# Loading and placing a table in two lots, and adding all row blocks of the output weight on GpSimd

## Chip, cores, metric

One core of a Trainium2 chip. The metric is the device time of one execution, in microseconds (us); "time" below is that, and "span" is the profiled execution from first to last instruction, some 1.5 to 2 us shorter.

## The reference, cut to what matters

```python
# x (8, 3008, 256), w_r/w_i (256, 256), w_in (256, 2048), w_out (2048, 256)
X  = rfft(x, axis=1)
Yr = Xr @ w_r - Xi @ w_i + b_r ;  Yi = Xr @ w_i + Xi @ w_r + b_i
Y  = soft-threshold(Yr, Yi, 0.01)
y  = irfft(Y)                       # (8, 3008, 256)
h  = relu(y @ w_in);  out = (s * h*h + b) @ w_out
```

The constant `b` contributes `b * (column sums of w_out)` to every row. The kernel computes that once, as a bias.

## The kernel before

The FFT over 3008 = 94 x 32 points is done with matmuls. Batch 0 goes first and alone, so its steps wait for each other: a first transform of the eight pieces of x (`ut`), a mix with the weights (`g`), a forward transform with tables `F_t` and `F_2`, relu steps (`m`, `z`), an inverse transform, transposes, a last transform. Mix, forward and inverse steps go in units of four pairs of frequencies; the result of each is copied out of PSUM by ScalarE or VectorE, which is called an eviction here. Then the big matmuls with `w_in` and `w_out` begin, with the later batches woven in. The tables of the first 12 of 24 pairs of frequencies come compactly (`F_c`) and are spread on the chip into zeroed blocks:

```python
    def emit_load_forward():
        nc.sync.dma_start(out=F_c.rearrange("p q r k -> p q (r k)"), in_=F_d)   # 192 KB
        nc.sync.dma_start(out=sel_t, in_=S_d)
    ...
    def place_f():                      # ScalarE
        for a in range(2):
            r = slice(64 * a, 64 * a + 64)
            nc.scalar.copy(out=blocks(F_t)[r, 0:H, :, a], in_=F_c[r])
    def place_f_2():                    # VectorE
        for a in range(2): ...          # two copies, two negations, 64x384 each
    ...
    # first_batch
        for g in range(8):              # two groups per chunk c of x, h = 0, 1
            ...                         # 8 matmuls on a piece of x, two evictions into ut
            last_pe = keep_awake(5)     # five filler matmuls
            if h == 0: continue
            if c == 0:
                with tc.issue_after(last_dve.ins):
                    nc.vector.memset(F_c[0:1, 0, 0, 0:1], 0.0)   # gate for the load
                emit_load_forward()
            ...
        with tc.issue_after(last_dve.ins), tc.issue_after(last_act.ins):
            place_f()
            place_f_2()
        ...
        for i in range(2 * U + 2):
            if i < 2 * U:          mix(*steps[i])
            if 0 <= i - 1 < 2 * U: fwd_dft(*steps[i - 1])
            if 0 <= i - 2 < 2 * U: inv_dft(*steps[i - 2])
```

`w_out` is loaded in two parts (12 and 4 of its 16 row blocks). GpSimd adds the first 12 blocks into two (`w_sum`, five adds), and six matmuls with a matrix of ones sum the rest over the partitions:

```python
    def make_bias():
        parts = [w_out_t[:, q] for q in range(12, MC)] + [w_sum[:, 0], w_sum[:, 1]]
        for i, part in enumerate(parts):
            nc.tensor.matmul(ps[:, 0:D], ones, part, ...)
        nc.scalar.activation(out=bias_bc, in_=ps[:, 0:D], func=AF.Copy, scale=bb_bc)
```

## Time and profile before

| | kernel before |
|---|---|
| time, first session | 847.06 us (846.77 to 847.17, 3 runs) |
| profiled span | 845.9 us (this execution took 847.72 us) |
| TensorE busy | 835.2 us, 99% |
| first mix matmul / first w_in matmul / first use of `us` | 14.39 / 46.05 / 62.97 us |

The three times of the last row are the marks: they cut the start into a stretch that x sets (to 14.39), the dependent steps of batch 0 (to 46.05) and the stretch in which the bias is made (to 62.97). The prediction shows the chain of waits and TensorE's timeline there. One line of the same timeline is needed further: the first inverse transform.

```profile
19.80 0.40 PE L478 MATMUL psa<-T_t,z 128*128 128x128 f16 x4
```

### The profile page before, as it was taken

The page shows a single profiled execution, that of the slowest core. Times are in us where ns is not written, and L with a number is a line of the kernel's source. Part 1 is how long each engine was busy: PE and PEld are TensorE (multiplying, and loading weights), DVE is VectorE, ACT ScalarE, POOL GpSimd, SP SyncE. Part 2 cuts the span into 40 slices and gives each one's busy share as a digit, 9 for nine tenths or more (in the row PEclk, how much of TensorE's full clock was granted, in tenths as well). Part 3 has the DMA queues.
Part 4 walks back from the last instruction along what each step waited for, and adds up shares of the span by engine and source line. Part 5 has one row for each costly group of instructions (what it writes and reads, how often), then busy time and mean ns, then how long its engine had stood idle before and what let it go on. Part 6 is the DMA issues. An engine that isn't in the chain of part 4 may idle for free.

```text
span 845.9 us, 17109 instructions
## 1 busy us (share of the span) xinstructions
PE 835.2 (99%) x6658; PEld 600.6 (71%) x6658; DVE 693.8 (82%) x1027; ACT 641.3 (76%) x862; POOL 42.9 (5%) x69
## 2 busy tenths in 40 slices
PE   8999999999999999999999999999999999999997
PEld 6857767777677767777677776777767777766765
DVE  5989987888888987888888888798978888776674
ACT  5988887778778877787777787778877778666673
POOL 4430000000000001000000000000000000000000
PEclk9999999999999999999999999999999999999999
DMA  8955467224762367324761247613354223411111
GB/s 199 175 153 121 117 161 205 68 73 102 194 163 57 101 166 197 85 73 107 189 173 50 81 100 198 168 44 90 102 155 122 61 79 97 112 33 38 38 44 50
DMA packets 105762, 96.06 MB, mean 114 GB/s; under 512 B 9558, under 2 KB 97498, under 8 KB 104338
## 3 DMA queue, kind: packets, MB, share of 16 engines
q1 hardware_dynamic: 99218, 80.55, 33.0%
q0 software_dynamic: 6464, 14.42, 10.6%
q8 instruction: 52, 0.85, 0.4%
q14 instruction: 28, 0.23, 0.1%
HBM read 53.52 MB, written 46.66 MB: 118 GB/s over the span
## 4 chain that ended last, share of the span: by engine, by line
PE 91%; DMA 3%; ACT 3%; DVE 2%; issue 1%; POOL 0%; DVEq 0%; ACTq 0%; POOLq 0%
PE psh L782 37%; PE psa L853 37%; PE psf L648 4%; PE psf L583 3%; PE psf L634 2%; PE psf L619 2%; PE psf L678 2%; PE psf L731 2%; ACT rt L789 1%; DMA ud<-u 1%; PE psm L430 1%; DMA x<-in_x_dram 1%; DMA F_c<-dft_fwd 1%; PE psf L460 0%; DMA ring<-ring 0%
## 5 line engine op out<-in xcount | busy, mean ns | idle before, releaser
L789 ACT ACTIVATE rt<-psh 128x1024 f32<-128x1024 f32 (+2 forms) x384 | 387.0, 1009 | 120.3 <-PE psh L782 119.1
L796 DVE TENSOR_TENSOR gt<-rt 128x1024 f16<-128x1024 f32 (+2 forms) x319 | 382.2, 1201 | 94.7 <-ACT rt L789 93.6
L853 PE MATMUL psa<-w_out_t,gt 128*128 128x256 f16 (+1 forms) x3024 | 454.1, 272 | 0.1
L853 PEld LDWEIGHTS <-gt 128*128 128x128 f16 (+1 forms) x3024 | 301.0, 101 | 186.1 <-issue 1.1
L782 PE MATMUL psh<-yt,w_in 128*128 128x512 f16 (+1 forms) x1344 | 396.6, 378 | 0.2 <-ACT rt L789 0.2
L782 PEld LDWEIGHTS <-w_in 128*128 128x128 f16 x1536 | 142.8, 98 | 26.3 <-issue 1.0
L863 DVE SCALAR_TENSOR_TENSOR ost<-psa,s_bc,bias_bc 128x512 f32<-128x512 f32 (+2 forms) x97 | 71.1, 733 | 9.6 <-PE psa L853 8.0
L793 ACT ACTIVATE gt<-rt 128x1024 f16<-128x1024 f32 (+2 forms) x65 | 68.2, 1050 | 1.0
L653 DVE TENSOR_TENSOR ring<-psf,s 128x512 f16<-128x512 f32 x84 | 57.5, 684 | 3.2 <-PE psf L648 2.9
L170 ACT CAST v<-psf 128x512 f16<-128x512 f32 x77 | 44.9, 582 | 19.3 <-PE psf L678 19.3
L170 ACT CAST xf<-psf 128x512 f16<-128x512 f32 x79 | 46.3, 586 | 9.4 <-PE psf L619 9.4
L782 PE MATMUL psh<-tail,w_in 128*128 128x512 f16 (+1 forms) x192 | 52.1, 353 | 0.0
L170 ACT CAST u<-psf 96x512 f16<-96x512 f32 x74 | 42.8, 580 | 11.3 <-PE psf L583 11.0
L648 PE MATMUL psf<-W_g,xf 128*128 128x256 f16 x336 | 50.4, 272 | 0.0
L170 ACT CAST yt<-psf 128x480 f16<-128x480 f32 (+2 forms) x76 | 38.9, 519 | 14.8 <-PE psf L731 14.2
L213 POOL DMA_DIRECT2D x<-in_x_dram x36 | 18.7, 526 | 433.2 <-PE psf L583 432.0
L583 PE MATMUL psf<-x,A_t 94*96 94x512 f16 x102 | 38.9, 382 | 1.0 <-ACT yt L170 0.6
L659 DVE TENSOR_TENSOR ring<-ring,high 128x512 f16<-128x512 f16 x84 | 35.5, 423 | 2.3
L660 DVE TENSOR_TENSOR ring<-ring 128x512 f16<-128x512 f16 x84 | 35.5, 423 | 2.1
L658 DVE TENSOR_TENSOR ring<-ring,low 128x512 f16<-128x512 f16 x84 | 35.4, 421 | 1.6
L648 PEld LDWEIGHTS <-xf 128*128 128x128 f16 x336 | 32.9, 98 | 4.1 <-issue 0.2
L731 PE MATMUL psf<-C_t,vs 96*128 96x96 f16 x448 | 33.2, 205 | 0.0
(99 smaller groups left out, 503.5 us busy)
## 6 DMA issues: line engine op xcount, KB each, us to landing
out_dram<-ost SPq DMA_DIRECT2D x152, 128.0 KB
ud<-u SPq DMA_DIRECT2D x28, 384.0 KB
us<-ud SPq DMA_DIRECT2D x28, 384.0 KB
vd<-v SPq DMA_DIRECT2D x42, 256.0 KB
vs<-vd SPq DMA_DIRECT2D x14, 768.0 KB
x<-in_x_dram POOLq DMA_DIRECT2D x28, 376.0 KB, 6.2
ring<-ring SPq DMA_DIRECT2D x280, 32.0 KB
out_dram<-ost SPq DMA_DIRECT2D x16, 120.0 KB
```

Of the source, the lines that this page charges most:

```text
L170: return None, nc.scalar.copy(out=dst, in_=src)
L583: nc.tensor.matmul(ps[0:96, :], A_t[0:N1, :], x16[(b, c)][0:N1, j * D : (j + 2) * D], start=True, stop=True,)
L648: nc.tensor.matmul(ps[:, r, :], xt[:, 2 - r, dc], W_g[:, dc, r], start=(dc == 0), stop=(dc == DC - 1),)
L653: nc.vector.tensor_tensor(out=t, in0=ps, in1=hold[i // 2][:, i % 2].unsqueeze(1).to_broadcast([P, 2, D]), op=ALU.add,)
L659: nc.vector.tensor_tensor(out=m, in0=m, in1=high, op=ALU.min)
L731: nc.tensor.matmul(ps[:, j * 96 : (j + 1) * 96], vs[(b, h)][:, k, ec * P : (ec + 1) * P], C_t, start=True, stop=True,)
L782: nc.tensor.matmul(o, w_in_t[dc][:, mc * P : (mc + 1) * P], r, start=(dc == 0), stop=(dc == DC - 1),)
L789: nc.scalar.activation(out=rt[:, :, 0:w], in_=ps[:, :, 0:w], func=AF.Relu)
L793: nc.scalar.activation(out=gt[:, :, 0:w], in_=rt[:, :, 0:w], func=AF.Square)
L796: nc.vector.tensor_tensor(out=gt[:, :, 0:w], in0=rt[:, :, 0:w], in1=rt[:, :, 0:w], op=ALU.mult)
L853: nc.tensor.matmul(ps[0:size, h, :], gts[(ti, mc // 2)][:, mc % 2, sub * size : (sub + 1) * size], w_out_t[:, mc, :], start=(mc == 0), sto ...
L863: nc.vector.scalar_tensor_tensor(out=ost[0:size, 0:k], in0=ps[0:size, 0:k], scalar=s_bc[0:size], in1=bias_bc[0:size].unsqueeze(1).to_broad ...
```

## The change

Intent: the first four pairs of the table are loaded at the very start and placed while TensorE waits for x, so that the first forward transform has nothing to wait for. The other eight pairs are placed behind the first mix unit. And `w_out` comes in four loads, so that GpSimd can add all 16 blocks as they land, which leaves two bias matmuls of six.

```diff
+    def load_f_c(q):
+        nc.sync.dma_start(out=F_c[:, q]..., in_=F_d[:, q])
+    load_f_c(slice(0, 4))                                   # 64 KB, no gate
     def emit_load_forward():
-        nc.sync.dma_start(out=F_c..., in_=F_d)
+        load_f_c(slice(4, H))                               # 128 KB
@@ w_out
-        for q in (slice(0, 12), slice(12, MC)):
+        for q in (slice(q, q + 4) for q in range(0, MC, 4)):
@@ zeroing of F_2[0]: four pairs on VectorE, eight on GpSimd
@@ placing
-    def place_f(): ...           def place_f_2(): ...
+    def place_f(q):
+        for a in range(2):
+            r = slice(64 * a, 64 * a + 64)
+            copy = nc.scalar.copy if a else nc.vector.tensor_copy
+            copy(out=blocks(F_t)[r, q, :, a], in_=F_c[r, q])
+            nc.vector.tensor_scalar_mul(... F_2[0] ..., scalar1=-1.0)
+            nc.vector.tensor_copy(... F_2[0] ...)
@@ sums
-        five adds over blocks 0 to 11
+        for q in range(2, MC, 2): nc.gpsimd.tensor_tensor(...)   # seven adds, all blocks
-        parts = [w_out_t[:, q] for q in range(12, MC)] + [w_sum[:, 0], w_sum[:, 1]]
+        for i in range(2): nc.tensor.matmul(ps[:, 0:D], ones, w_sum[:, i], ...)
@@ first_batch
             if c == 2: ...
+                with tc.issue_after(last_dve.ins), tc.issue_after(last_act.ins):
+                    place_f(slice(0, 4))
-        place_f(); place_f_2()
+            if i == 0:                                       # behind mix unit 0
+                with tc.issue_after(left[0].ins), tc.issue_after(left[1].ins):
+                    place_f(slice(4, H))
```

More of the change, by code (lines that the diff above doesn't have):

```diff
@@ L264 @@
     T_t = cpool.tile([P, NPAIR, P], F16, name="T_t")
+    def load_f_c(q):
+        nc.sync.dma_start(out=F_c[:, q].rearrange("p q r k -> p q (r k)"), in_=F_d[:, q])
+    load_f_c(slice(0, 4))
     def emit_load_forward():
-        nc.sync.dma_start(
-            out=F_c.rearrange("p q r k -> p q (r k)"), in_=F_d
-        )
+        load_f_c(slice(4, H))
         nc.sync.dma_start(out=sel_t, in_=S_d)
@@ L300 @@
     nc.vector.memset(F_t[:, 0:H], 0.0)
-    nc.gpsimd.memset(F_2[0], 0.0)
+    nc.vector.memset(F_2[0][:, 0:4], 0.0)
+    nc.gpsimd.memset(F_2[0][:, 4:H], 0.0)
     def make_bounds():
@@ L321, in place_w @@
             nc.scalar.copy(out=W_t[:, :, i], in_=w_st[i])
-    def place_f():
+    def place_f(q):
         for a in range(2):
             r = slice(64 * a, 64 * a + 64)
-            nc.scalar.copy(out=blocks(F_t)[r, 0:H, :, a], in_=F_c[r])
-    def place_f_2():
-        for a in range(2):
-            r = slice(64 * a, 64 * a + 64)
+            copy = nc.scalar.copy if a else nc.vector.tensor_copy
+            copy(out=blocks(F_t)[r, q, :, a], in_=F_c[r, q])
             nc.vector.tensor_scalar_mul(
-                out=blocks(F_2[0])[r, :, 0, a], in0=F_c[r, :, 1], scalar1=-1.0
+                out=blocks(F_2[0])[r, q, 0, a], in0=F_c[r, q, 1], scalar1=-1.0
             )
-            nc.vector.tensor_copy(out=blocks(F_2[0])[r, :, 1, a], in_=F_c[r, :, 0])
+            nc.vector.tensor_copy(out=blocks(F_2[0])[r, q, 1, a], in_=F_c[r, q, 0])
     w_sum = cpool.tile([P, 2, D], F16, name="w_sum")
@@ L342, in sum_w_out @@
         acc = opool.tile([P, 2, D], F32, name="acc", tag="ost")
-        nc.gpsimd.tensor_tensor(
-            out=acc, in0=w_out_t[:, 0:2], in1=w_out_t[:, 2:4], op=ALU.add
-        )
-        for q in (4, 6, 8):
-            nc.gpsimd.tensor_tensor(out=acc, in0=acc, in1=w_out_t[:, q : q + 2], op=ALU.add)
-        nc.gpsimd.tensor_tensor(out=w_sum, in0=acc, in1=w_out_t[:, 10:12], op=ALU.add)
+        for q in range(2, MC, 2):
+            nc.gpsimd.tensor_tensor(
+                out=w_sum if q == MC - 2 else acc, in0=acc if q > 2 else w_out_t[:, 0:2],
+                in1=w_out_t[:, q : q + 2], op=ALU.add,
+            )
     def make_bias():
         ps = other_bank()
-        parts = [w_out_t[:, q] for q in range(12, MC)] + [w_sum[:, 0], w_sum[:, 1]]
-        for i, part in enumerate(parts):
-            nc.tensor.matmul(
-                ps[:, 0:D], ones, part, start=(i == 0), stop=(i == len(parts) - 1)
-            )
+        for i in range(2):
+            nc.tensor.matmul(ps[:, 0:D], ones, w_sum[:, i], start=(i == 0), stop=(i == 1))
         nc.scalar.activation(out=bias_bc, in_=ps[:, 0:D], func=AF.Copy, scale=bb_bc)
@@ L395, in first_batch @@
                 with tc.issue_after(last_dve.ins):
-                    nc.vector.memset(F_c[0:1, 0, 0, 0:1], 0.0)
+                    nc.vector.memset(F_c[0:1, 4, 0, 0:1], 0.0)
                 emit_load_forward()
@@ L405, in first_batch @@
                     place_w()
-        with tc.issue_after(last_dve.ins), tc.issue_after(last_act.ins):
-            place_f()
-            place_f_2()
         gate = nc.gpsimd.tensor_copy(out=w_in_t[0][0:1, 0:1], in_=F_t[0:1, H, 0:1])
@@ L435, in mix @@
                 if half:
-                    nc.scalar.copy(out=g[:, 2:4], in_=ps)
+                    on_act = nc.scalar.copy(out=g[:, 2:4], in_=ps)
                     load["act"] += 0.58
                 else:
-                    nc.vector.tensor_tensor(
+                    on_dve = nc.vector.tensor_tensor(
                         out=g[:, 0:2], in0=ps,
@@ L446, in mix @@
                     load["dve"] += 0.69
+            return on_dve, on_act
         def fwd_dft(ec, u):
@@ L535, in first_batch @@
             if i < 2 * U:
-                mix(*steps[i])
+                left = mix(*steps[i])
+            if i == 0:
+                with tc.issue_after(left[0].ins), tc.issue_after(left[1].ins):
+                    place_f(slice(4, H))
             if 0 <= i - 1 < 2 * U:
```

## The prediction

> **What bounds the kernel now.** I read the page first: its busy shares, then the idle before each group. Then the chain of waits in its first 70 us, because the diff touches only the start, and last the timeline of those stretches engine by engine.
>
> ```profile
> PE 835.2 (99%) x6658; PEld 600.6 (71%) x6658; DVE 693.8 (82%) x1027; ACT 641.3 (76%) x862; POOL 42.9 (5%) x69
> PE 91%; DMA 3%; ACT 3%; DVE 2%; issue 1%; POOL 0%; DVEq 0%; ACTq 0%; POOLq 0%
> ```
>
> TensorE is busy for 835.2 of 845.9 us, so only 10.7 us of idle time is left in the whole span, and the chain that ended last is TensorE for 91%. All matmul work of the main part stays as it is. The change can therefore win only from two things: the few idle microseconds at the start, and the four matmuls that it takes away. The table of windows puts the idle time of TensorE at 2.25 us in 0 to 10, 1.6 us in 10 to 20, 0.2 us in 20 to 40 and 0.9 us in 40 to 50 us; the rest is spread thinly and lies at the very end. What the diff aims at is in the chain of waits of 5 to 20 us (columns: start, length, what):
>
> ```profile
> 2.89 6.68 DMA x<-in_x_dram
> ...
> 10.77 4.42 DMA F_c<-dft_fwd
> ...
> 15.27 0.83 ACT F_t L326
> ...
> 16.11 0.83 ACT F_t L326
> ...
> 16.96 0.59 ACT g L436
> ...
> 17.60 0.38 PE psf L460 x4
> 17.98 0.87 PE psm L430 x8
> ```
>
> The reader is to see that between 10.77 and 17.60 us the end of the kernel is held by the table F_c: issued at 10.77, landed at 15.19, spread into F_t by two ScalarE copies of 0.83 us, which in turn hold back the eviction g. TensorE's own timeline shows the cost (start, length, line, count, idle before and who ended it):
>
> ```profile
> 14.39 1.92 PE L430 MATMUL psm<-W_t,ut 128*128 128x256 f16 x16
> 17.00 0.23 PE L460 MATMUL psf<-g,F_t 128*128 128x128 f16 x1 [0.69 <-ACT F_t L326]
> ...
> 17.60 0.22 PE L460 MATMUL psf<-g,F_t 128*128 128x128 f16 x1
> ...
> 17.82 1.04 PE L430 MATMUL psm<-W_t,ut 128*128 128x256 f16 x8
> ```
>
> The first two mix units run from 14.39 to 16.31, then TensorE waits 0.69 us for F_t and a further part of the next 0.6 us for g. From 17.82 on it is full: in 20 to 30 us it is busy for 10.00 of 10.00 us. So the delay at 16.3 us is passed on whole.
>
> The second place is the bias, at 52 to 55 us:
>
> ```profile
> 52.63 0.38 PE L354 MATMUL psa<-w_out_t,ones 128*128 128x256 f16 x2
> 52.94 1.02 PE L782 MATMUL psh<-yt,w_in 128*128 128x512 f16 x4
> ...
> 54.02 0.38 PE L354 MATMUL psa<-w_out_t,ones 128*128 128x256 f16 x2
> 54.24 0.38 PE L354 MATMUL psa<-w_sum,ones 128*128 128x256 f16 x2
> ```
>
> Each pair occupies TensorE for 0.22 us (54.02 to 54.24), that is 0.11 us for one, although a single record lasts 0.27 us: the records overlap. ScalarE in this stretch shows no idle time from 47.24 to 57.95 us.
>
> **What the Trainium skill says.** "VectorE: DVE Perf Modes", section "The perf-mode tier table": a 16-bit tensor_copy or tensor_scalar within SBUF can run faster than one element a cycle, while an operand in PSUM drops a tier. The trace agrees: a 64x384 f16 placement on VectorE takes 0.25 us, a 128x384 eviction from PSUM 0.56 us. "SBUF — State Buffer" tells of one port pair that VectorE and GpSimd share, and of an exclusive lock. The trace shows no harm to evictions from PSUM: VectorE's 96x512 casts take 0.68 us during GpSimd's adds (40.6 to 46.7 us) and 0.69 us outside (30.27). "DMA: Bandwidth & Descriptors", section "Issuing engines are not separate DMA queues": transfers of all issuers interleave on the same 16 engines. The windows agree: the DMA share is 1.03 to 1.15 in 6.5 to 12.5 us, while TensorE waits for x. "Perfetto Trace Analysis", section "DMA Optimizations", says that splitting a DMA lets some work start sooner if the engines are otherwise idle; between 20 and 40 us they are not (share 0.7 to 1.4), which speaks for a small gain from the four loads alone.
>
> **Part 1, tables of four pairs early.** A third of F_c (64 of 192 KB) is issued at about 3.6 us, behind the bias loads, and lands long before 12 us. These four pairs are placed after the third chunk of x, near 12 to 13 us: on ScalarE one 64x256 copy, on VectorE one 64x256 copy and four 64x128 operations. From the present rows: ScalarE 0.83 us for 768 elements, with some 0.17 us fixed, gives 0.17 + 0.22 = 0.39 us. VectorE 0.25 us for 384, with some 0.06 fixed, gives 0.19 us for 256 and 0.13 us for each of four, 0.7 us in all, or 0.55 us by starts that overlap as they do now. These are estimates. VectorE has idle gaps of 0.34 to 0.43 us in front of each ut cast here, ScalarE about 0.5 us. So the work fits in two gaps, and may push the last VectorE cast (14.03 to 14.59 us) by 0.1 us. That cast feeds the first mix unit, so I charge **+0.1 us**. The 64 KB now travel while DMA is full with x; at the 200 GB/s that the windows show they take 0.32 us, but part of the old 192 KB also ran beside the last chunks of x. I charge half, **+0.15 us**.
>
> Gain: the first forward transform no longer waits for F_c. Its g: the first half of mix unit 0 is complete near 15.0 us, plus 0.69 us on VectorE gives 15.7; the second half near 15.45, plus 0.58 us on ScalarE gives 16.03. Both are ready before TensorE ends the 16 mix matmuls at 16.31. A forward unit takes 0.56 us (18.69 to 19.25). So the third mix unit starts at 16.31 + 0.56 = 16.87 in place of 17.82: **-0.95 us**.
>
> **Part 2, the other eight pairs behind the first mix unit.** 128 KB issued at 10.77 as before, landed by about 15. VectorE is free at 15.7: one 64x512 copy (0.33) and four 64x256 (0.19 each), 0.9 us by starts, so to 16.6. ScalarE from 16.03: 0.17 + 0.44 = 0.61, to 16.65. Then the evictions of mix unit 1: VectorE to 17.3, ScalarE to 17.25. TensorE needs them after the third mix unit (eight matmuls, 0.87 us): at 16.87 + 0.87 = 17.74. Slack 0.4 us, so this part is hidden. The first relu then ends near 17.9 and its VectorE step near 18.6, before the first inverse transform that I expect at 18.8 (19.80 now).
>
> **Part 3, w_out in four loads.** The sums are seven GpSimd adds of 1.23 us by starts in place of five, and four matmuls fewer. The loads land at 40.6 and 41.9 us now (issue plus 19.3 and 19.6). w_in has landed by about 35, so four quarters land near 36.8, 38.5, 40.2 and 41.9; seven adds from 36.9 end at about 45.5 (46.7 now), 7 us before the bias needs them. Two more issues cost GpSimd about 1.1 us at 23 us, where it is idle. TensorE loses 4 x 0.11 = 0.44 us of work. The first pair is worth nothing where it stands: the matmul at 52.94 could not start before the second-last relu ended (51.82 + about 1.02 = 52.84) and its signal came. Of the rest ScalarE, full until 57.95, eats some. I keep half: **-0.2 us**.
>
> **Sum.** -0.95 + 0.1 + 0.15 - 0.2 = -0.9 us, so 847.06 - 0.9 = **846.1 us**. Evictions bound the stretch of 32 to 46 us (VectorE is full there), but their work is the same and starts earlier, so the shift passes through. The round trip of u through DRAM (us<-ud landed near 60.5, first used at 62.97) moves with it.
>
> **Rivals.** (a) A new wait for the one removed: if the placement of the first four pairs also waits for the later F_c load, VectorE stands still from 12.6 to 15 us with the last ut casts behind it, and the kernel gets 1.5 to 2 us slower, about 848.8. Against it: TensorE reads F_t's first half at 17.00, while GpSimd's gate on the second half is released only at 17.59, so halves of a tile are told apart. (b) The x stream, which DMA bounds, is delayed by the full 64 KB and the four early copies delay the last casts more: -0.4 us in all, 846.7. For it: a DMA share above 1.0 up to 12.5 us. (c) The shift is lost later at a fixed arrival, for instance the weights or us: 846.9. Against it: no TensorE wait for a weight appears, and only 0.7 us of waits for us<-ud in all. (d) The order of instructions changes further on and closes some later gap, or the bias is worth its full 0.44 us: 845.2.
>
> **Range and chances.** The base case is 846.1; (b) and (d) lie 0.6 to 0.9 us off, and reordering of thousands of instructions can add as much again. I give 844.6 to 847.4. Two per cent is 17 us, more than all idle time of TensorE, so faster by 2% is about impossible; slower by 2% would need a broken overlap that lasts.
>
> **What would show it.** Right: no TensorE idle of 0.69 us behind the first 16 mix matmuls; the third mix unit about 0.9 us earlier; F_c off the chain of waits; the first w_in matmul (46.05 now) near 45.1; two bias matmuls in place of six; w_sum ready before 47 us. Wrong: VectorE idle before 15 us for F_c, the first mix matmul later than 14.7 us, or a start that is 0.9 us early with an end that is not.

## The result, and the profile after

| same session | time | runs |
|---|---|---|
| before | 847.33 us (846.77 to 847.56) | 6 |
| after | 846.49 us (846.18 to 847.06) | 6 |

The ratio of after to before is 0.9991, with a 95% interval of 0.9978 to 1.0004. The time lies inside the predicted range, 0.4 us above the predicted 846.1. The interval includes 1: these runs alone do not show that the change is faster.

The page of the changed kernel, its span and its chain by line:

```profile
span 844.6 us, 17119 instructions
...
PE psa L852 38%; PE psh L781 37%; PE psf L647 4%; PE psf L582 3%; PE psf L633 2%; PE psf L677 2%; PE psf L618 2%; PE psf L730 2%; ACT rt L788 1%; DMA x<-in_x_dram 1%; PE psm L425 1%; POOL x L213 0%; ACT yt L170 0%; DVE z L463 0%; PE psf L456 0%
```

F_c has left the list of the chain. TensorE's timeline (start, length, line, count, idle before and who ended it), the changed kernel:

```profile
13.77 0.34 PE L374 MATMUL psm<-A_t,x 94*128 94x96 f16 x4 [0.28 <-DMA x<-in_x_dram]
...
14.68 1.92 PE L425 MATMUL psm<-W_t,ut 128*128 128x256 f16 x16
16.44 0.22 PE L456 MATMUL psf<-g,F_t 128*128 128x128 f16 x1
...
16.99 1.04 PE L425 MATMUL psm<-W_t,ut 128*128 128x256 f16 x8
...
19.31 0.40 PE L474 MATMUL psa<-T_t,z 128*128 128x128 f16 x4 [0.20 <-DVE z L463]
```

The wait of 0.69 us for F_t is gone: the forward transform follows the 16 mix matmuls at once, and the third mix unit starts at 16.99 in place of 17.82. Two things are less good. The last piece of x, and with it the first mix matmul, came 0.29 us later (14.68 against 14.39). And at the first inverse transform TensorE now waits 0.20 us for z: it starts at 19.31, only 0.49 us before the 19.80 of before.

ScalarE and VectorE in the same stretch of the changed kernel, two views:

```profile
15.98 0.59 ACT L431 CAST g<-psm 128x512 f16<-128x512 f32 x1 [1.36 <-PE psm L425]
16.59 0.61 ACT L332 COPY F_t<-F_c 64x512 f16<-64x512 f16 x1
17.23 0.59 ACT L431 CAST g<-psm 128x512 f16<-128x512 f32 x1
17.84 0.69 ACT L461 ACTIVATE m<-psf,neg_lam 128x512 f32<-128x512 f32 x1
```

```profile
13.93 1.02 DVE L174 CAST ut<-psf 128x384 f16<-128x384 f32 x2
15.65 0.69 DVE L434 TENSOR_TENSOR g<-psm,b_g 128x512 f16<-128x512 f32 x1 [0.70 <-PE psm L425]
...
18.56 0.69 DVE L463 SCALAR_TENSOR_TENSOR z<-psf,m 128x512 f16<-128x512 f32 x1
```

The late copy of 0.61 us stands on ScalarE between two evictions g; the relu m comes last, and z waits for it. VectorE's last ut cast ends at 14.95, after the first mix matmul has started.

The bias in the changed kernel:

```profile
52.13 0.38 PE L352 MATMUL psa<-w_sum,ones 128*128 128x256 f16 x2
```

Two matmuls in place of six; as before, they don't hold TensorE for all of their busy time: it goes on with the next matmuls at 52.45, 0.32 us after their start.

**Where the 1.3 us between the two profiled spans lie.** I cut both traces at the marks and, further on, at GpSimd's issues of x and its copies of the tail, which stand in the same order in both. Each difference is after minus before:

| stretch | before | after | difference |
|---|---|---|---|
| start to first mix matmul | 14.39 | 14.68 | +0.29 |
| to first w_in matmul | 31.66 | 30.88 | -0.78 |
| to first use of `us` | 16.92 | 16.76 | -0.16 |
| to first x load of batch 3 | 32.79 | 32.80 | +0.01 |
| to its second x load | 15.33 | 15.11 | -0.22 |
| to the fourth tail copy | 430.53 | 430.53 | 0.00 |
| to the fifth tail copy | 100.94 | 100.55 | -0.39 |
| to the end | 203.34 | 203.29 | -0.05 |

The instruction lists of the two built kernels show that nothing else moved: ScalarE's and VectorE's lists differ only by the evictions and placements of the start, TensorE's only by the bias matmuls and by two w_in matmuls beside them. So -0.65 us of the profiled 1.3 lie in the five stretches that the change did not mean to touch. The -0.39 of the fifth tail copy is most likely the single execution's: that stretch is 100.94 and 100.77 us in the two profiles of the kernel before, 100.72 in rest_later, and 100.54 or 100.55 in the eleven others, sum_only with its old start among them. Which other parts belong to the change and which to the single execution is what the experiments have to tell.

### The profile page after: what moved, and what is told of

Read it like the earlier page. It is cut to its first block, busy times and chain, and to the rows that moved or that the text cites. A ratio compares the mean times of both kernels' runs of the same rounds, so it can differ in the third digit from the quotient of the medians.

```text
span 844.6 us, 17119 instructions
## 1 busy us (share of the span) xinstructions
PE 835.1 (99%) x6654; PEld 601.3 (71%) x6654; DVE 694.7 (82%) x1034; ACT 640.6 (76%) x862; POOL 45.9 (5%) x73
## 3 DMA queue, kind: packets, MB, share of 16 engines
q0 software_dynamic: 6496, 14.42, 10.6%
## 4 chain that ended last, share of the span: by engine, by line
PE 92%; ACT 3%; DVE 2%; DMA 1%; issue 1%; POOL 0%; DVEq 0%; ACTq 0%; POOLq 0%
PE psa L852 38%; PE psh L781 37%; PE psf L647 4%; PE psf L582 3%; PE psf L633 2%; PE psf L677 2%; PE psf L618 2%; PE psf L730 2%; ACT rt L788 1%; DMA x<-in_x_dram 1%; PE psm L425 1%; POOL x L213 0%; ACT yt L170 0%; DVE z L463 0%; PE psf L456 0%
```

## The experiments

My theory after reading the result: the tables are worth some 0.5 us, the bias 0.15 us, the rest is jitter of arrivals. Rivals: only the bias counts; all of it is jitter of x; the early table load delays x.

All profiles, cut at the same marks (us; "third mix" is the start of the third mix unit after the first mix matmul):

| run | first mix | third mix | first mix to first w_in | first w_in to first `us` |
|---|---|---|---|---|
| before | 14.39 | 3.43 | 31.66 | 16.92 |
| before_again | 14.36 | 2.91 | 31.13 | 16.93 |
| sum_only (old start) | 14.26 | 2.96 | 31.18 | 16.76 |
| after | 14.68 | 2.31 | 30.88 | 16.76 |
| after_again | 14.42 | 2.31 | 30.88 | 17.13 |
| early_only | 15.88 | 2.32 | 30.88 | 16.91 |
| rest_later | 14.20 | 2.32 | 30.88 | 16.76 |
| rest_again | 14.26 | 2.40 | 30.97 | 16.76 |
| act_free | 14.35 | 2.31 | 30.92 | 16.76 |
| all_early | 14.73 | 2.40 | 30.97 | 16.81 |
| awake | 15.43 | 2.31 | 30.88 | 16.77 |
| cold | 14.67 | 3.66 | 31.89 | 16.77 |
| split_late | 14.07 | 2.32 | 31.16 | 16.76 |
| first_later | 16.30 | 4.46 | 33.28 | 16.76 |

### 1. The two halves apart: early_only and sum_only

`early_only` is the change with w_out and the bias as before; `sum_only` is the kernel before with the four loads, seven adds and two bias matmuls.

> Parts 1 and 2 of the change (tables of four pairs early, eight placed behind the first mix unit), with w_out in two loads and the bias in six matmuls as before. My account (the start gives about 0.5 us where the main part begins, the bias 0.15 us, the rest of the gain in the profiled run is jitter of arrivals later on): about 0.5 us under the kernel before, first w_in matmul at 45.5 to 45.7 us, L619-type first forward unit of batch 1 about 0.5 us earlier than the 62.97 of before. Rival (the start is worth nothing in the end, the whole gain is the bias): same time as before.

> Part 3 alone on the kernel before: four loads of w_out, seven GpSimd adds, two bias matmuls. My account: the four matmuls are 0.44 us of TensorE, of which ScalarE's relu chain eats most: 0.1 to 0.25 us faster than before; first w_in matmul unchanged at 46.05. Rival (TensorE is the bound there, all of it counts): 0.44 us faster. Rival (the additional adds come too late): slower.

Measured: before 847.20 us (846.85 to 849.06, 9 runs); early_only 847.22 (846.58 to 848.35, 5 runs), ratio 0.9999 (0.9985 to 1.0013); sum_only 846.89 (846.76 to 846.92), ratio 0.9993 (0.9981 to 1.0006).

The bias is settled by the marks: from the first w_in matmul to the first use of `us` it is 16.91 to 16.93 us in the three profiles with six matmuls (before, before_again, early_only) and 16.76 to 16.81 with two, but for after_again (below). So it is worth 0.16 us, where the four matmuls occupied 0.44 us.

The tables alone gave no time here. The profiled run (848.0 us, the second slowest of the five) shows where it lost. Its stretch from the first mix matmul to w_in is 30.88 us, as good as in the change. But its first mix matmul came only at 15.88. TensorE's timeline in early_only:

```profile
13.86 0.53 PE L378 MATMUL psm<-A_t,x 94*128 94x96 f16 x4
...
14.98 0.34 PE L378 MATMUL psm<-A_t,x 94*128 94x96 f16 x4
...
15.88 1.92 PE L429 MATMUL psm<-W_t,ut 128*128 128x256 f16 x16
```

A group of four matmuls takes 0.53 us at 13.86, and 0.34 at 14.98. The profile names no DMA for the last group, which stands behind the slow ones. But x was late too. The packed trace keeps, for each transfer, when each of its 16 parts was reported as landed (no view prints this). The last part of x's last piece landed at 14.65 us here, against 13.30 to 13.43 in the three profiles with the old start. Where TensorE stood ready, it started 0.04 or 0.05 us after that landing, so x alone would have put the last group at 14.70. The slow groups cost 0.28 us of the delay, the late piece the rest. The windows of the same run give a granted clock of 0.50 from 9 to 14 us. In the changed kernel's own profile the same happened for a shorter time. Its windows (stretch, length, busy time of PE, PEld, DVE, ACT, POOL, granted clock, DMA share, GB/s):

```profile
8.00:9.00 1.00, 0.70 (x15) 0.53 (x13) 0.56 (x2) 0.39 (x2) 1.00 (x2) 0.95 1.15 217
9.00:10.00 1.00, 1.00 (x15) 0.95 (x13) 0.56 (x1) 0.45 (x1) 0.19 (x1) 0.50 1.13 205
...
11.00:12.00 1.00, 1.00 (x14) 1.00 (x12) 0.45 (x1) 0.95 (x3) 0.00 (x0) 0.50 1.06 200
```

There it ended early enough for the last piece of x to be the bound again (0.28 us of wait for x at 13.77), so it cost nothing that this profile shows. The Trainium skill, "TensorE: Matmul & The Clock Gate", section "HAM oscillation — how this bites in real kernels", puts a fall of the clock down to idle gaps over some 3.4 us. In these two profiles the longest gaps ahead of the fall were 1.12 us (after) and 0.84 us (early_only), so here shorter ones went before it.

### 2. The load of the other eight pairs against x: rest_later

In the changed kernel the gate of this load stands on VectorE after two evictions; in the kernel before it stood after four. SyncE issued it at 8.66 us in place of 10.77. The source has the gate behind the first chunk of x (`c == 0`) in both kernels; the order on VectorE is read from the traces, and why it came out differently is not on record. The experiment puts it back:

```diff
-            if c == 0:
+            if c == 1:
                 with tc.issue_after(last_dve.ins):
                     nc.vector.memset(F_c[0:1, 4, 0, 0:1], 0.0)
                 emit_load_forward()
```

> The change with the load of the other eight pairs gated on the second chunk of x in place of the first, so that its gate stands behind four evictions as in the kernel before. In the changed kernel this load was issued at 8.66 us (10.77 before) and the last piece of x came 0.30 us later. Theory that this load delays x: last piece of x back at about 13.45, first mix matmul at 14.4, and the kernel 0.2 to 0.3 us faster than the change. Rival (the 64 KB issued at 3.67 us delay x, or x just varies): last piece of x stays near 13.77 and the time is that of the change.

Measured: 846.15 us (845.89 to 847.53), ratio to before 0.9989 (0.9976 to 1.0001). SyncE issued the load at 10.65 us again. TensorE's lines in rest_later:

```profile
13.29 0.34 PE L374 MATMUL psm<-A_t,x 94*128 94x96 f16 x4 [0.17 <-DMA x<-in_x_dram]
...
14.20 1.92 PE L425 MATMUL psm<-W_t,ut 128*128 128x256 f16 x16
```

The change itself was first compared side by side in section 6. The last piece of x came earlier, as expected by the theory that this load delays it, and the eight pairs still land in time (30.88 us to w_in). It was repeated (section 6).

### 3. The late copy on ScalarE: act_free

```diff
-            copy = nc.scalar.copy if a else nc.vector.tensor_copy
+            copy = nc.scalar.copy if a and q.start == 0 else nc.vector.tensor_copy
```

> The change with the late placement of F_t's second half of rows on VectorE too, so that ScalarE places nothing behind the first mix unit. In the changed kernel ScalarE's copy of 0.61 us stands between the two evictions g and the first relu waits for it; TensorE then waits 0.20 us for z at 19.3. Theory that this copy holds the path: first inverse transform 0.3 to 0.5 us earlier against the first mix matmul, and the time 0.2 to 0.4 us under the change. Rival (VectorE's additional 0.27 us holds its own eviction and z as long): same as the change within 0.15 us.

Measured: 847.05 us (846.17 to 848.09), ratio 0.9996 (0.9984 to 1.0009). TensorE in act_free:

```profile
16.66 1.04 PE L425 MATMUL psm<-W_t,ut 128*128 128x256 f16 x8
...
18.38 0.60 PE L425 MATMUL psm<-W_t,ut 128*128 128x256 f16 x4
19.03 0.40 PE L474 MATMUL psa<-T_t,z 128*128 128x128 f16 x4
```

The wait for z is gone, but the fourth mix unit starts 1.72 us after the third in place of 1.52: VectorE, with 0.27 us more to place, held its own eviction. From the first mix matmul to the inverse transform it is 4.68 us against 4.63 in the change, and to w_in 30.92 against 30.88. The rival was right, by this profile: the placement behind mix unit 0 costs about the same on either engine.

### 4. The clock in the x stretch: cold and awake

`cold` has one filler matmul behind each piece of x, `awake` has 16 and 10 behind the first two and five behind the others.

```diff
-                last_pe = keep_awake(5)
+                last_pe = keep_awake(1)                             # cold
+                last_pe = keep_awake({0: 16, 1: 10}.get(g, 5))      # awake
```

> The change with one filler matmul behind each piece of x in place of five, made slower on purpose. In the profiles so far TensorE's groups of four matmuls on x took 0.53 us in place of 0.34 for a stretch after idle gaps of 0.84 to 1.12 us (granted clock 0.88 in 0 to 14 us in the changed kernel, first mix matmul at 14.68; at 15.88 in the run with the tables early alone). Theory that idle gaps in this stretch lower the clock and that this lower clock costs time: groups of 0.5 us in most of 7 to 14 us, first mix matmul at 15.5 to 16.5 us, 0.7 to 1.7 us slower than the change. Rival (x's arrival alone sets the first mix matmul): 13.8 to 14.7 us and the time of the change.

> The change with 16 and 10 filler matmuls behind the first two pieces of x in place of five each, to fill the gap in which TensorE waits for the second and third piece. If the lower clock is what spreads the times of the change: all groups of 0.34 us from 7 us on, first mix matmul at 14.1 to 14.5, times within 0.5 us of each other near 846.1. Rival (the clock in this stretch costs nothing): median and spread as in the change (846.2 to 847.1).

Measured: before 846.91 us (846.62 to 847.42, 9 runs); cold 848.83 (847.50 to 849.07), ratio 1.0022 (1.0008 to 1.0036); awake 847.74 (847.24 to 848.79), ratio 1.0011 (0.9999 to 1.0024).

cold is slower, clear of noise, but not in the place that I had named. TensorE in cold:

```profile
13.60 0.50 PE L374 MATMUL psm<-A_t,x 94*128 94x96 f16 x4 [0.26 <-DMA x<-in_x_dram]
...
14.67 3.27 PE L425 MATMUL psm<-W_t,ut 128*128 128x256 f16 x16
```

x still sets the first mix matmul; it is the 16 mix matmuls that take 3.27 us in place of 1.92. So in this run slow matmuls while waiting for x did no harm until they reached past the last piece: there they cost 1.35 us, of which 1.01 are left at the first w_in matmul (31.89 against 30.88). In early_only they cost 0.28 us by piling up.

The slow rate of cold is not a fall. The first piece's group of x takes 0.50 us in the kernel before too (at 5.92 us), and 0.34 from the second piece on; in cold all eight take 0.50, from the first at 5.62. The windows read a granted clock of 1.00 throughout both, so the profile's clock does not show this slow rate. The profiled run of cold (847.50) is also the fastest of its five. The other four (848.18 to 849.07) have mean clocks of 0.993 or 0.994 against its 1.000, so they lost something that this profile can't show.

awake refutes my hope. All groups but the first took 0.34 us, as expected, but the last piece of x came late, and all five runs are slower than the median of before. TensorE in awake:

```profile
14.51 0.34 PE L374 MATMUL psm<-A_t,x 94*128 94x96 f16 x4 [1.05 <-DMA x<-in_x_dram]
```

The last piece came at 14.51 there, with TensorE idle for 1.05 us. Fifteen of its 16 parts had landed by 13.83 us and the last only at 14.47 (13.87 and 14.65 in early_only). Why one part lags so is open; the load of the eight pairs was issued at 8.39 us, as early as in the change.

### 5. The early load: all_early and first_later

`all_early` loads the whole F_c at 3.5 us. `first_later` gates the four pairs on the first chunk of x and the eight on the second.

```diff
-    load_f_c(slice(0, 4))
+    load_f_c(slice(0, H))                       # all_early, no second load
```

```diff
-    load_f_c(slice(0, 4))
...
             if c == 0:  ...gate...; load_f_c(slice(0, 4))      # first_later
             if c == 1:  ...gate...; load of slice(4, H)
```

> The change with the whole table F_c (192 KB) loaded at 3.5 us in place of 64 KB there and 128 KB at 8.7 us: three times the suspected cost. Theory that the early load takes DMA time from the first pieces of x: second and third piece of x later by a further 0.3 to 0.6 us (8.0 in place of 7.5 us), a longer idle gap, lower clock more often; 0.3 to 1.5 us slower than the change. Rival (the early load is free): same as the change.

> The change with the load of the first four pairs gated on the first chunk of x (issued near 8.5 us) and that of the other eight on the second (near 10.6 us), so that neither runs beside the first pieces of x. Theory that the early load opens the gap before the second piece: TensorE idle there 0.25 us as in the kernel before (0.68 to 1.12 us in the four profiles with the early load), no stretch of lower clock, first mix matmul at 14.1 to 14.4; 0.2 to 0.6 us under the change and a narrower spread, unless the first four pairs then land after 12.4 us and VectorE waits for them. Rival (the gap varies by itself): gap of 0.7 us or more here too.

Measured in the call of cold and awake: all_early 846.53 us (846.03 to 846.96), ratio 0.9996 (0.9983 to 1.0008); first_later 847.53 (847.31 to 850.72), ratio 1.0016 (1.0003 to 1.0029).

The theory that the early load holds up the first pieces of x finds no support: with three times the bytes the second piece was used at 6.91 us, against 7.50 in the change and 7.47 in the kernel before. And the gap before the second piece is not the early load's doing: first_later, without it, shows 0.94 us, and the second look at the kernel before shows 1.30 us.

The last piece is another matter. TensorE's line in all_early:

```profile
13.82 0.34 PE L373 MATMUL psm<-A_t,x 94*128 94x96 f16 x4
```

Its last part had landed at 13.77 us, as late as in the change (13.72), though nothing of F_c was issued at 8.7 us. So a second load at 8.7 us isn't the only thing that can make it late. Over the 14 profiles the last part landed at 13.39 to 14.65 us in the seven with the whole table issued before 10 us, at 13.11 to 13.30 in the four with only the 64 KB issued by then, and at 13.30 to 13.43 in the three with none. A late piece goes with the whole table being issued early; how the one delays the other is open.

first_later shows what the early issue is good for. Its profiled run (850.72) is the slowest of the five, 2.5 us above the next, so the sizes below are not those of a typical run. ScalarE and TensorE in first_later:

```profile
14.96 0.40 ACT L330 COPY F_t<-F_c 64x256 f16<-64x256 f16 x1 [3.04 <-DMA F_c<-dft_fwd]
```

```profile
16.30 3.60 PE L426 MATMUL psm<-W_t,ut 128*128 128x256 f16 x16 [2.22 <-ACT ut L170]
```

The 64 KB, issued at 8.32 us behind x, landed just before 14.96, some 6.6 us later; fifteen of its 16 parts were there by 13.61 us, the last at 14.88. ScalarE and VectorE stood still with the last ut casts behind the placement, TensorE idled for 2.22 us, and its granted clock reads 0.50 from 16 to 22 us. This is the stall of the prediction's rival (a), brought about in another way (there the placement would have waited for the later load): the placement ahead of the last casts is safe only because its data are there.

### 6. Once more, side by side: after_again, rest_again, split_late, before_again

`after_again`, `rest_again` and `before_again` are unaltered repeats of the change, of rest_later and of the kernel before. `split_late` is rest_later with the eight pairs in two lots:

```diff
             if i == 0:
-                    place_f(slice(4, H))
+                    place_f(slice(4, 8))
             ...  done = fwd_dft(*steps[i - 1])
+            if i == 1:
+                with tc.issue_after(done[0].ins), tc.issue_after(done[1].ins):
+                    place_f(slice(8, H))
```

> The change once more, unaltered, to be compared with the next runs on one chip and as a further profile. My account: first mix matmul anywhere from 14.2 to 15.9 us, by x's last piece and by whether TensorE's clock falls in 7 to 14 us; from there to the first w_in matmul 30.88 us as in every profile with early tables so far (31.66 in the kernel before); 0.3 to 1.0 us under the kernel before. Rival (the 30.88 is luck of those runs): over 31.2.

> The kernel with the later load of the other eight pairs, repeated beside the change. If that load at 8.7 us delays x's last piece: 0.2 to 0.4 us under the change again, and last piece of x before 13.5 us. Rival (that run was lucky): equal to the change within 0.2 us.

> As rest_again, with the eight later pairs placed in two lots: four behind the first mix unit, four behind the first relu step and its VectorE step. It takes 0.2 us from ScalarE and 0.4 us from VectorE ahead of the first relu. Theory that the late placement costs the 0.2 us wait of TensorE for z at the first inverse transform: no such wait, from the first mix matmul to the first w_in matmul 30.6 to 30.75 us. Rival (the wait moves to the second or third unit): 30.85 or more.

> The kernel before, one further look. From the first mix matmul to the third mix unit 3.43 us in the first profile, 2.96 in the run of the sums alone, which has the same start: it hangs on when F_c lands after x. Expected 2.9 to 3.6 us, and 31.1 to 31.8 us from the first mix matmul to the first w_in matmul; if it comes to under 31.0, the gain at the start is luck.

Measured (but nine of the ten runs of before are those of the preceding call, on the same chip): before 846.92 us (846.62 to 847.42, 10 runs); after_again 846.83 (846.30 to 846.91), ratio 0.9998 (0.9984 to 1.0012); rest_again 846.35 (846.21 to 846.50), ratio 0.9994 (0.9981 to 1.0006); split_late 846.34 (846.16 to 846.92), ratio 0.9995 (0.9982 to 1.0009); before_again, one run, 847.39.

before_again tells most about the size of the gain. Its TensorE:

```profile
14.36 1.92 PE L430 MATMUL psm<-W_t,ut 128*128 128x256 f16 x16
16.44 0.23 PE L460 MATMUL psf<-g,F_t 128*128 128x128 f16 x1 [0.15 <-ACT F_t L326]
...
17.27 1.04 PE L430 MATMUL psm<-W_t,ut 128*128 128x256 f16 x8
```

The wait for F_t that the prediction set out to remove is 0.15 us here, 0.21 us in sum_only and 0.69 us in the one profile that I had. In all three, fifteen of F_c's 16 parts had landed by 13.83 to 14.04 us; the last came at 14.62, 14.58 and 15.19. So the wait hangs on one late part, and the profile that I had was a late one.

after_again lost 0.37 us between w_in and `us`: ScalarE waited 0.86 us for a buffer u to be written out (released by the store to DRAM), which no other profile shows.

rest_again holds up: each of its five runs lies below each of the ten of before, though it overlaps with after_again (846.21 to 846.50 against 846.30 to 846.91). The last piece of x was used at 13.29, 13.34 and 13.16 us in the three profiles with the later load (rest_later, rest_again, split_late). With the load at 7.9 to 8.7 us it was 13.77, 13.51, 13.43, 14.51 and 13.60 (after, after_again, act_free, awake, cold), and in early_only it landed at 14.65. With the old start it was 13.47, 13.45 and 13.35. split_late started its first inverse transform 4.42 us after the first mix matmul, without a wait, but lost it again: the second lot stands on VectorE behind z, the second inverse transform came at 6.17 (6.08 in rest_later), the third at 7.83 (7.53), and w_in at 31.16 against 30.88. The rival was right again.

## Why the prediction was right, step by step

The total and the range held, but the terms of the sum did not each hold: that they came so near the total is in part luck.

**Start, -0.95 us.** The mechanism held: no wait for F_t, F_c off the chain, the third mix unit 2.31 us after the first mix matmul where I had 2.48. The size did not. This term is the one that was mis-sized, for two reasons.
- It was worked out against one execution. In the three profiles with the old start the stretch to w_in takes 31.66, 31.13 and 31.18 us; 30.88 us in both profiles of the change. So the gain is 0.25 to 0.78 us. I had read 0.69 us of wait off one profile as if it were the kernel's own, and that execution (847.72 us) was slower than the runs whose median I subtracted from.
- The step "part 2 is hidden" failed in part. The evictions of mix unit 1 were in time for TensorE, as predicted, but I had the first relu end at 17.9 and z at 18.6, in time for the inverse transform. Shifted by the 0.29 us that x was late, that is 18.2 and 18.9; they ended at 18.53 and 19.25. I had the halves of mix unit 0 ready 0.6 and 1.06 us after the first mix matmul; their evictions began after 0.97 and 1.30, most likely because the mix also needs VectorE's last ut cast, which ended 0.27 us after the first mix matmul. Of 0.6 us won at the third mix unit (2.91 or 2.96 against 2.31) 0.3 us is left at the inverse transform (4.89 or 4.94 against 4.63).

**Early placement and x, +0.25 us.** The sign held in the profile (+0.29), the reason did not. The first pieces of x were not held up, as all_early shows; the last piece most likely was, by the whole table being issued before 10 us (sections 5 and 6). The 128 KB came that early because their gate moved up from behind four evictions to behind two, which the prediction had overlooked ("issued at 10.77 as before"). Slow matmuls, which cost 1.35 us where they reached the mix in cold, were in no term at all. They may be part of the spread of the runs: in act_free the two runs with mean clocks of 0.995 and 0.997 are the slowest (847.75 and 848.09). But the change's own run with 0.997 took 846.48, its median. The landing of x's last piece, 13.11 to 14.65 us over the profiles, is the larger spread that they show.

**Bias, -0.2 us.** It measured -0.16 us. The argument, that ScalarE is full there and eats the rest, fits (its busy stretch ends at 58.02 in the trace, not at 57.95). The loads were issued later than I had (25.69 and 27.54 us for the third and fourth, where I had all by about 24), and w_sum was done at 46.07 and not 45.5, still 6 us before its use. GpSimd in the changed kernel:

```profile
25.69 0.75 POOL L296 DMA_DIRECT2D w_out_t<-in_moe_w_out_dram  x1 [3.04 <-DMA x<-in_x_dram]
27.54 0.74 POOL L296 DMA_DIRECT2D w_out_t<-in_moe_w_out_dram  x1 [1.10 <-DMA x<-in_x_dram]
...
44.91 1.16 POOL L344 TENSOR_TENSOR w_sum<-acc,w_out_t 128x512 f16<-128x512 f32 x1
```

**The shift passes through.** Right: from the first inverse transform to w_in it is 26.25 us before and 26.25 after. Rival (c), a loss at a fixed arrival, or one like it, happened in one profile (0.37 us in after_again).

**What was in no step.** Between two x loads of batch 3 the change gains 0.23 us: 15.33 to 15.35 us in the three profiles with the old start, 15.10 or 15.11 in all eleven with the tables placed in lots. It is one VectorE instruction that starts 0.58 us after the one ahead of it in place of 0.35. VectorE in sum_only, then in the changed kernel:

```profile
106.61 0.42 DVE L655 TENSOR_TENSOR ring<-ring,high 128x512 f16<-128x512 f16 x1
107.19 0.69 DVE L649 TENSOR_TENSOR ring<-psf,s 128x512 f16<-128x512 f32 x1 [0.16 <-DMA ring<-ring]
```

```profile
106.73 0.42 DVE L658 TENSOR_TENSOR ring<-ring,high 128x512 f16<-128x512 f16 x1
107.08 0.68 DVE L652 TENSOR_TENSOR ring<-psf,s 128x512 f16<-128x512 f32 x1
```

The profile puts it down to a DMA, but in rest_again the same transfers were issued 0.9 us later against this instruction and nothing waited. The kernels without the delay have six or more instructions more on VectorE ahead of it; why that should matter is open.

**What the change is worth.** By the profiles 0.25 to 0.78 (start), 0.16 (bias) and 0.23 us, less what x loses. By the times -0.84 us in one session and -0.09 in another. Put together, 11 runs of the change have a median of 846.51 us, and 26 of the kernel before one of 847.02. So about half a microsecond, not clear of noise, with the gain of a single session from nearly nothing to twice that. rest_later looks like the better form of it: 846.35 us over ten runs. Neither differs from before by an interval that leaves out 1.

## What to carry to other kernels

A wait read off one profile is one draw: where it ends with a DMA landing, look at a second execution before the whole of it is booked as gain. Work that is moved off one wait must be followed to the next consumer on the same engine; here half of what the third mix unit won (0.3 of 0.6 us) was gone two steps later, and moving the work to another engine or in time gave nothing back. When a load is split, look at where the gates of its parts land in the issuing order: the second part moved up by 2 us unasked, and putting it back looks worth about as much as the change itself (846.83 to 846.35 us; the runs of the two overlap).

## What the Trainium skill lacked or had wrong

- "TensorE: Matmul & The Clock Gate", section "HAM oscillation — how this bites in real kernels", speaks of idle gaps over some 3.4 us. Here the granted clock fell to 0.50 for about 3 to 6 us in a stretch whose longest gaps were 0.84 us (early_only) and 1.12 us (after); 1.30 us in before_again brought no fall. The length of one gap did not decide it. The page tells elsewhere of falls by frequent short gaps, but gives no length or busy share for them.
- "DMA: Bandwidth & Descriptors", section "Specifications", gives a first-byte latency of about 0.6 us for SyncE's transfers, and no figure for one behind a backlog. In first_later 64 KB from SyncE, issued behind GpSimd's loads of x, took some 6.6 us to land (8.32 to 14.88), the last of its 16 parts 1.27 us after the fifteenth.
- No page has it: a VectorE instruction that starts 0.23 us later or not, the same in each of the 14 profiles, by what stands far ahead of it in its list (15.33 to 15.35 us against 15.10 to 15.11).
